# Block-sparse attention with a Fourier mixer: the mask's factors in one room, GpSimd adds the last units, and three smaller moves

## The chip, the cores and the metric

The kernel runs on one core of one Trainium2 chip. A core has TensorE (PE, with its weight loads shown as PEld), VectorE (DVE), ScalarE (ACT), GpSimd (POOL) and SyncE (SP), which issues most of the DMAs. The metric is the device time of one launch in microseconds (us), as the median of several executions; lower is better. One further execution was recorded by the hardware profiler. Its span is the time from its first to its last instruction, and all times inside the kernel are counted from the start of that span.

## What is computed

Attention over 4 batches of 8 heads, 768 positions and 64 elements a head, with a mask on blocks of 32 x 32 positions; then a Fourier mixer over the joined heads.

```python
scores = scale * np.matmul(q, k.transpose(0, 1, 3, 2))
mask = np.abs(blk_i - blk_j) <= window            # + first/last block rows and columns
for qb in range(n_blocks):
    for kb in sampled_blocks[qb]:                  # 3 random blocks for each block of queries
        mask[qb*block:(qb+1)*block, kb*block:(kb+1)*block] = True
attn = softmax(np.where(mask, scores, -1e9));  x = attn @ v      # (4, 8, 768, 64)
x = x.transpose(0, 2, 1, 3).reshape(4, 768, 512)
u = x + np.real(np.fft.fft(np.fft.fft(x, axis=1), axis=2))
un = (u - mean) / np.sqrt(var + 1e-6)
out = u + np.maximum(un @ w_ch1, 0) @ w_ch2        # w_ch1 512 x 2048, w_ch2 2048 x 512
```

The mask depends on the random blocks, so it is built on the chip from `sampled_blocks`.

## The kernel before

**Units, slots and batches.** Two heads make a pair; there are 16 pairs, four in each batch. A pair has 12 units: two halves of 384 queries by six chunks `c` of 128 keys. Two units make a slot, six slots a pair and 24 slots a batch. The function `slot(sl)` (96 attention slots and then the rest) issues a slot's work for all engines in program order. In each slot TensorE computes the scores of two units (`scores`, L570, 4 matmuls each), ACT takes the exponential to `e` (`weigh`), and a slot or two later TensorE multiplies `e` with the values (`values`, L633). The loop also puts in work of other kinds from queues: `short` (turning the next q and k with TensorE, L503; placing finished outputs, `xt` L657; totals), `apart` and `late` (the mixer of the batch before). Where these go is decided while the program is written out: the code keeps modelled times of each engine (`when`, `busy`) and of each PSUM bank (`free`, `give`), and takes the first item that is ready by this model. So a change of one cost, bank or queue can move other instructions too.

**The mask, in two ways.** In the first, TensorE adds a large negative number to forbidden scores: the mask as a product of two bf16 factors, `of_k` (24 rows that say which block a key is in, kept twice at rows 0 and 64) and `off_q`, accumulated into the scores' PSUM bank (L580, "factor products"); then one exponential (L590) gives `e`. In the second, ACT takes the exponential in place (L593) and DVE multiplies it by a uint8 mask (L595). The first is used for the whole first batch and on, until `go()` ends it (L1311 to 1313) when the first mixer's channels begin. The uint8 mask is computed in batch 0 by 12 `mask_step`s (L355 to 364): one matmul of the two factors over 24 rows into bank "m" (L361), and a cast by ACT (L363), one in each slot from 4 to 15.

**Where the factors are.** They are made in two tiles of the tag "acc", which later hold the sums of `e`. At the end of slot 19, `keep_factors` (L475 to 480) has POOL copy both into room 2 of a set of big rooms (`big0` to `big5`), for use from slot 20 on. Until then the six rooms are a ring for weight chunks: each of 32 chunks of 512 KB is loaded by SP (`w_load`, L441) into room `i % 6`, then split for rounding by two ACT instructions (L450, L453) and five DVE ones (L454 to L462), 1.42 chunks a slot. A load needs its room's former chunk to be rounded.

**Sums of the exponentials.** In batch 0 TensorE adds `e` over the keys (`add_up`, L701). From pair 4 on, `gather` adds each unit to a running sum `acc` for its half: POOL in two halves of 384 elements (L619), or DVE in one instruction of 768 (L614), chosen by the model's times; only units masked by TensorE may go to DVE. For those units `gather` is called in `values`, a slot after the exponential; for the others right after the DVE multiply. In the second slot of the next pair at the latest `total` (L715) sums both halves over the keys with TensorE, into bank "t", and DVE adds the result to the batch's sums.

**Turning.** `turn` (L486 to 519) turns q or k of a pair with TensorE (L503) into a PSUM bank, "t" or "m", which `turn_on` names, and ACT or DVE copies it out.

**The last outputs.** For the last batch, `outputs` (L1124 to 1190) forms each 128-row block `m` of the outputs by 256-column products (L1151), that DVE adds to `xA` and `xB` (L1158). `plus(b1, p5)` and `plus(b0, ...)` complete the two column halves of a block of the second sequence half, and `plus(a1, p3)` the first half's. `store` (L1096 to 1101) then writes whole rows of 512 columns from SP, as one or two DMAs by the order in which the rows lie.

Of the kernel before, what the change touches and what calls it, by code (L numbers as in the profile page):

```python
# [102 lines left out]
def kernel(  # L103
# [101 lines left out]

    HOP = 0.1

    pairs = [(b, j) for b in range(B) for j in range(NP)]
    loaded, v_of = {}, {}

# [113 lines left out]
                                pattern=pat)  # L324


    at_k = acc_p.tile([P, 2, 2 * HS], BF16, tag="acc", name="at_k")
    at_q = acc_p.tile([P, 2, 2 * HS], BF16, tag="acc", name="at_q")
    of_k, off_q, keep_q = at_k[:, 0, :], at_q[:, 0, :], at_q[:, 1, :]

    nc.vector.memset(of_k, 0.0)
    nc.vector.memset(off_q, 0.0)

    def twice(t):
        nc.vector.tensor_copy(out=t[D:D + NB, :], in_=t[0:NB, :])
# [20 lines left out]
    twice(off_q)  # L356
    def mask_step(i):

        half, c = divmod(i, C)
        m, at = ps_m.tile([P, 512], FP32, tag="m", name="m"), bank("m")  # L360
        nc.tensor.matmul(m[:, 0:HS], of_k[0:NB, c * P:(c + 1) * P],  # L361
                         keep_q[0:NB, half * HS:(half + 1) * HS], start=True, stop=True)
        nc.scalar.copy(out=mask[:, c, half * HS:(half + 1) * HS], in_=m[:, 0:HS])  # L363
        give(at, busy("ACT", 0.5, busy("PE", 0.2) + HOP))


    def table_s(src, dst, t):
# [64 lines left out]
                              ap=[[2 * cols, P], [1, 2 * WN]])  # L432
                wchunks.append((src, w_sb[:, row, col:col + WN]))
    wraw = {}
    ROOMS = 6
    def room(i, shape, name, dtype=FP32):
        return big.tile(shape, dtype, tag=f"big{i}", name=name)

    def w_load(i):
        t = room(i % ROOMS, [P, 3 * WN], "wraw", U32)  # L440
        nc.sync.dma_start(out=t[:, 0:2 * WN].bitcast(I32), in_=wchunks[i][0])  # L441
        wraw[i] = t

# [25 lines left out]

    by_pe = set()
    factors = {"at": (of_k, off_q)}

    def keep_factors():  # L475

        kept = room(2, [P, 2, S], "factors", BF16)
        for a, t in enumerate(factors["at"]):
            nc.gpsimd.tensor_copy(out=kept[:, a, :], in_=t)
        factors["at"] = kept[:, 0, :], kept[:, 1, :]  # L480

    turned, e_of, acc_of, o_of, sums_of, x_of, sp_of = {}, {}, {}, {}, {}, {}, {}
    s_at, e_at, e_free, oT_at, acc_at = {}, {}, {}, {}, {}

    def turn_on(n, a, half):
        return "m" if n > NP and (a, half) == (0, 1) else "t"  # L486

    def turn(n, a, half):

# [63 lines left out]
    def scores(us):  # L553

        n, w = divmod(us[0], UP)
        half = w // C
        qT, kT = turned[n, 0], turned[n, 1]
        queries = slice(half * HS, (half + 1) * HS)
        got = []
        for u in us:  # L560
            c = u % C
            s = ps_s.tile([P, 2, 512], FP32, tag="s", name="s")
            got.append((u, s))
            if n < NP or (factors["at"] and True):
                by_pe.add(u)
            busy("PE", 0.72, max(e_at.get(u - SLOT, 0.0), z_at[u % 2]))
            s_at[u] = when["PE"] + HOP
            for i in range(2):
                rows = slice(D * i, D * i + D)
                nc.tensor.matmul(s[:, i, 0:HS], kT[rows, c * P:(c + 1) * P], qT[rows, queries],  # L570
                                 start=True, stop=u not in by_pe)
        for u, s in got:
            if u not in by_pe:
                continue
            c, (at_k, at_q) = u % C, factors["at"]
            busy("PE", 0.25)
            s_at[u] = when["PE"] + HOP
            for i in range(2):
                rows = slice(D * i, D * i + D)
                nc.tensor.matmul(s[:, i, 0:HS], at_k[rows, c * P:(c + 1) * P], at_q[rows, queries],  # L580
                                 start=False, stop=True)
        return got

    def weigh(u, s):
        n, w = divmod(u, UP)
        half, c = divmod(w, C)
        e = ep.tile([P, 2, HS], FP32, tag="e", name="e")
        e_of[u] = e
        if u in by_pe:
            nc.scalar.activation(out=e, in_=s[:, :, 0:HS], func=ACT.Exp, scale=scale)  # L590
            e_at[u] = busy("ACT", 0.8, max(s_at[u], e_free.pop(u - 2 * SLOT, 0.0))) + HOP
        else:
            nc.scalar.activation(out=s[:, :, 0:HS], in_=s[:, :, 0:HS], func=ACT.Exp, scale=scale)  # L593
            m = mask[:, c, half * HS:(half + 1) * HS].rearrange("p (o s) -> p o s", o=1)
            nc.vector.tensor_tensor(out=e, in0=s[:, :, 0:HS], in1=m.broadcast_to([P, 2, HS]),  # L595
                                    op=ALU.mult)
            e_at[u] = busy("DVE", 0.97, busy("ACT", 0.8, s_at[u]) + HOP) + HOP
            if n >= NP:
                gather(u)

    def gather(u):


        n, w = divmod(u, UP)
        half, c = divmod(w, C)
        if c == 0:
            return
        if c == 1:
            acc_of[n, half] = acc_p.tile([P, 2, HS], FP32, tag="acc", name="acc")
        acc, e = acc_of[n, half], e_of[u]  # L610
        start = e_of[u - 1] if c == 1 else acc
        at = max(e_at[u], acc_at.get((n, half), 0.0))
        if u in by_pe and factors["at"] and max(when["DVE"], at) + 1.0 < max(when["POOL"], at) + 2.9:
            nc.vector.tensor_tensor(out=acc, in0=start, in1=e, op=ALU.add)  # L614
            acc_at[n, half] = busy("DVE", 1.0, at) + HOP
        else:

            for i in range(2):
                nc.gpsimd.tensor_add(out=acc[:, i, :], in0=start[:, i, :], in1=e[:, i, :])  # L619
            acc_at[n, half] = busy("POOL", 2.9, at) + HOP  # L620
        e_free[u] = acc_at[n, half]

    def values(u):
        n, w = divmod(u, UP)
        half, c = divmod(w, C)
        e = e_of[u]
        busy("PE", 0.75, e_at[u])
        vt = v_of[n]
        if c == 0:
            o_of[n, half] = ps_o.tile([P, HS], FP32, tag="o", name="o")  # L630
        o = o_of[n, half]
        for i in range(2):
            nc.tensor.matmul(o[D * i:D * i + D, :], vt[:, i, c, :], e[:, i, :],  # L633
                             start=(c == 0), stop=(c == C - 1))
        if u in by_pe and n >= NP:
            gather(u)
        if c == C - 1:
            if half == 1:
                v_of.pop(n)
            oT = sum_p.tile([P, HS], FP32, tag="oT", name="oT")  # L640
            if in_blocks(n):
                nc.vector.transpose(out=oT, in_=o_of.pop((n, half)))
                oT_at[n, half] = busy("DVE", 0.5, when["PE"] + HOP) + HOP
# [299 lines left out]
    def mixer(b, xA, xB):  # L943
# [149 lines left out]
            if r == NF // 4 - 1:  # L1093
                store(half, m)

        def store(half, m):  # L1096
            x = (xA, xB)[half]
            for p0, cnt, rows in _rows(out[b], T * half + m):
                nc.sync.dma_start(out=rows, in_=x[p0:p0 + cnt, m, :])
            if m == T - 1:  # L1100
                finished.add((b, half))

# [34 lines left out]
        def outputs(r, m, after):  # L1137
# [43 lines left out]
               in1=u.rearrange("p (o d) -> p o d", o=1).broadcast_to([P, 2, DH]), op=ALU.add)  # L1181
            busy("DVE", 0.7)
            plus(b1, p5)
            ahead(2)
            plus(b0, product(ps_s, "s", a22, rights[4]))
            if r == 1:
                store(1, m)
            ahead(3)
            p3 = product(ps_m, "m", o_s[m, 4], block(r, 1, 1))
            plus(a1, p3)  # L1190
            if r == 1:
                store(0, m)
            ahead(4)

        fl = [[("tm"[h == 1 and m != 1], lambda h=h, m=m: un_flip(h, m), 0.6, 0.55, 0.0)
               for m in range(T)]
# [105 lines left out]
    def begin(b):  # L1302
# [7 lines left out]

        def go():  # L1311
            late.extend(rest)
            factors["at"] = None
        apart.append(("-", go, 0.0, 0.0, 0.0, hold))

    def rest():
# [7 lines left out]
        return True  # L1324

    def w_loads():
        while state["got"] < min(len(wchunks), state["w"] + ROOMS):
            w_load(state["got"])
            state["got"] += 1

# [5 lines left out]
    def slot(sl):  # L1336
# [23 lines left out]
        got = scores(units) if sl < B * SB else ()  # L1360
        if paired and len(due) == 2:
            sum_up()
        for u, ps in got:
            weigh(u, ps)
        if BY_VECTOR <= n + 1 < len(pairs):
            for at, fn, args in ((0, squares, (n + 1, 0)), (1, flip_blocks, (n + 1, 0)),
                                 (2, in_order, (n + 1,)), (4, flip_blocks, (n + 1, 1)),
# [50 lines left out]
        if sl == 0:  # L1418
            short.append(("t", 0.0, lambda: turn(0, 1, 1)))
        if sl == 1:  # L1420
            short.append(("t", 0.0, lambda: turn(0, 0, 1)))
        if phase == 0 and 4 <= sl < 4 + 2 * C:
            short.append(("m", 0.0, lambda: mask_step(sl - 4)))
        if r > 0 and 0 < phase and not needed.intersection(map(id, short)) and once("mixing", phase):
            begin(phase - 1)
        left = SB * (phase + (0 if r == 0 else 1)) + 1 - sl
# [24 lines left out]
            item[2]()  # L1451
        w_loads()
        w_steps(sl)
        if sl == SB - 5:
            keep_factors()
        if sl >= 4 and sl % 2 == 0:
            table_step()

# [139 lines left out]
```

## Time and profile before

| | us |
|---|---|
| median of 3 executions | 1077.72 (1076.29 to 1078.42) |
| the profiled execution | 1078.02 |
| its span | 1075.9 |
| mean granted TensorE clock | 0.991 |
| factor products L580 on the kept factors, x108 | 14.0 busy, 6.1 idle before them |
| factor products L580 on the first tiles, x80 | 9.8 |
| mask matmuls L361, x12 | 4.0 |
| ACT mask casts L363, x12 | 5.9 |
| POOL adds L619, x150 and x44 | 152.1 and 48.2 |
| DVE adds L614, x21 | 20.8 |
| DVE mask multiplies L595, x98 | 89.1 |

The page gives the busy time of each engine, the span in 40 slices (26.9 us each, in tenths; the row PEclk is the granted clock of TensorE), the DMA queues, the chain of work that ended last, the groups of instructions by line, and the DMA issues. A group's line names the engine, the operation, output and inputs, how often it ran, its busy time and the mean of one, and then the idle time of the engine just before these instructions with what ended it. Queries of the trace give the waits, the timeline of a stretch, and the engines' busy time by stretch. The time of the profiled execution is about 2.1 us longer than its span.

### The profile page before, as it was taken

Reading aid. Unit: us, or ns where it says so; the run is one execution under the profiler, and the core shown is the slowest. Engines: PE = TensorE matmul, PEld = TensorE weight load, DVE = VectorE, ACT = ScalarE, POOL = GpSimd, SP = SyncE. Lnnn points to the kernel's source line nnn. Section 1 sums busy time; section 2 is a strip of 40 time slices with the busy share of each in tenths; the row PEclk is TensorE's granted clock in tenths of the full one; section 3 lists DMA queues with packets and bytes.
Section 4 is the critical chain, followed back from the end, with each engine's and each line's share of the span. In section 5 each row is a group of like instructions: output and inputs, shape, how many; then the busy total and the mean of one; then the engine's idle time right before and its main releaser. Section 6 shows DMA issues by size and latency. Waiting matters only on the chain.

```text
span 1075.9 us, 12388 instructions
## 1 busy us (share of the span) xinstructions
PE 1042.7 (97%) x4378; PEld 536.5 (50%) x4378; DVE 665.4 (62%) x1226; ACT 375.7 (35%) x742; POOL 231.1 (21%) x258
## 2 busy tenths in 40 slices
PE   8999898999999999999999999999999999999996
PEld 4433344444355555444444555443444555568575
DVE  5899694776771644664568446565556364675663
ACT  5998664563411202353352202243330302210210
POOL 1000080332700001256455001354630001000000
PEclk9999898999999999999999999999999999999998
DMA  7757230220100001222211000221000001000001
GB/s 225 222 176 240 58 71 15 45 45 16 29 1 1 0 1 30 59 38 42 54 27 33 0 1 10 69 40 31 15 8 8 0 1 30 30 1 1 1 18 44
DMA packets 120481, 46.65 MB, mean 43 GB/s; under 512 B 108110, under 2 KB 113244, under 8 KB 120412
## 3 DMA queue, kind: packets, MB, share of 16 engines
q1 hardware_dynamic: 118524, 44.99, 17.0%
q10 hardware_dynamic: 1856, 0.79, 0.3%
q8 instruction: 36, 0.59, 0.2%
q14 instruction: 33, 0.27, 0.1%
q0 software_dynamic: 32, 0.01, 0.0%
HBM read 37.11 MB, written 6.29 MB: 40 GB/s over the span
## 4 chain that ended last, share of the span: by engine, by line
PE 88%; DVE 7%; ACT 2%; issue 2%; POOL 1%; DMA 0%; ACTq 0%; DVEq 0%; POOLq 0%
PE y L1088 22%; PE z L1032 15%; PE s L570 12%; PE o L633 10%; PE yp L1032 7%; PE yy L1151 6%; PE xp L1032 4%; PE zp L842 2%; PE sp L701 1%; PE s L580 1%; PE zp L814 1%; PE utp L957 1%; DVE x L743 1%; PE sp L715 1%; PE tp L503 1%
## 5 line engine op out<-in xcount | busy, mean ns | idle before, releaser
L619 POOL TENSOR_TENSOR acc<-acc,e 128x384 f32<-128x384 f32 x150 | 152.1, 1050 | 85.3 <-DVE e L595 83.2
L570 PE MATMUL s<-qT,kT 64*128 64x384 f32 x768 | 154.4, 518 | 3.3 <-DVE e L595 1.9
L633 PE MATMUL o<-e,vr 128*64 128x384 f32 x768 | 142.8, 500 | 0.0
L1088 PE MATMUL y<-w_sb,hB 128*128 128x512 f32 x288 | 128.6, 596 | 1.4 <-DVE x L1091 1.4
L1088 PE MATMUL y<-w_sb,hA 128*128 128x512 f32 x288 | 129.2, 595 | 0.0
L1091 DVE TENSOR_TENSOR x<-y,x 128x512 f32<-128x512 f32 x72 | 49.7, 690 | 121.4 <-PE y L1088 121.2
L595 DVE TENSOR_TENSOR e<-s,mask 128x768 f32<-128x768 f32 x98 | 89.1, 950 | 56.8 <-ACT s L593 46.9
L593 ACT ACTIVATE s<-s 128x768 f32<-128x768 f32 x98 | 74.3, 792 | 93.3 <-PE s L570 93.0
L570 PEld LDWEIGHTS s<-qT,kT 64*128 64x128 f32 x768 | 64.3, 187 | 79.0 <-issue 24.1
L1032 PE MATMUL z<-unT,t 128*128 128x384 f32 x256 | 93.1, 486 | 0.7 <-DVE hA L1037 0.7
L590 ACT ACTIVATE e<-s 128x768 f32<-128x768 f32 x94 | 71.6, 814 | 47.7 <-PE s L580 33.9
L1088 PEld LDWEIGHTS y<-w_sb,hB 128*128 128x128 f32 x288 | 53.3, 190 | 67.3 <-issue 64.0
L905 POOL TENSOR_SCALAR st<-st 128x1 f32<-128x1 f32 x24 | 8.8, 365 | 355.2 <-DVE st L904 355.1
L1037 DVE TENSOR_TENSOR hA<-z,hA 128x384 f32<-128x384 f32 x64 | 35.7, 557 | 79.8 <-PE z L1032 79.8
L633 PEld LDWEIGHTS o<-e,vr 128*64 128x64 f32 x768 | 48.3, 137 | 71.6 <-issue 68.6
L1088 PEld LDWEIGHTS y<-w_sb,hA 128*128 128x128 f32 x288 | 53.1, 190 | 61.5 <-issue 58.4
L619 POOL TENSOR_TENSOR acc<-e 128x384 f32<-128x384 f32 x44 | 48.2, 1115 | 127.1 <-PE sp L715 93.6
L1041 ACT ACTIVATE hA<-hA 128x384 f32<-128x384 f32 x64 | 33.5, 523 | 119.0 <-DVE hA L1037 118.6
L1032 PEld LDWEIGHTS z<-unT,t 128*128 128x128 f32 x256 | 48.6, 190 | 35.0 <-DVE hA L1037 1.3
L1041 ACT ACTIVATE hB<-hB 128x384 f32<-128x384 f32 x64 | 33.5, 523 | 87.0 <-DVE hB L1037 87.0
L1052 ACT COPY hA<-xp 128x384 f32<-128x384 f32 x32 | 15.3, 478 | 107.0 <-PE xp L1032 107.0
L1032 PE MATMUL z<-t,w_sb 128*128 128x384 f32 x128 | 46.7, 488 | 0.9 <-DVE t L994 0.9
(206 smaller groups left out, 1439.2 us busy)
## 6 DMA issues: line engine op xcount, KB each, us to landing
wraw<-in_moe_w_ch_dram SPq DMA_DIRECT2D x32, 512.0 KB
vr<-in_v_dram SPq DMA_DIRECT2D x30, 192.0 KB
qb<-in_q_dram SPq DMA_DIRECT2D x44, 96.0 KB
kb<-in_k_dram SPq DMA_DIRECT2D x44, 96.0 KB
x<-oT SPq DMA_DIRECT2D x192, 12.0 KB
out_dram<-x SPq DMA_DIRECT2D x16, 128.0 KB
out_dram<-x SPq DMA_DIRECT2D x8, 256.0 KB
qr<-in_q_dram SPq DMA_DIRECT2D x24, 64.0 KB
```

Of the source, the lines that this page charges most:

```text
L570: nc.tensor.matmul(s[:, i, 0:HS], kT[rows, c * P:(c + 1) * P], qT[rows, queries], start=True, stop=u not in by_pe)
L590: nc.scalar.activation(out=e, in_=s[:, :, 0:HS], func=ACT.Exp, scale=scale)
L593: nc.scalar.activation(out=s[:, :, 0:HS], in_=s[:, :, 0:HS], func=ACT.Exp, scale=scale)
L595: nc.vector.tensor_tensor(out=e, in0=s[:, :, 0:HS], in1=m.broadcast_to([P, 2, HS]), op=ALU.mult)
L619: nc.gpsimd.tensor_add(out=acc[:, i, :], in0=start[:, i, :], in1=e[:, i, :])
L633: nc.tensor.matmul(o[D * i:D * i + D, :], vt[:, i, c, :], e[:, i, :], start=(c == 0), stop=(c == C - 1))
L1032: nc.tensor.matmul(to, a[:, k, :], c[:, k, :], start=(k == 0), stop=(k == ND // 2 - 1))
L1037: tt(out=to, in0=ps, in1=a, op=ALU.add)
L1041: nc.scalar.activation(out=h, in_=h, func=ACT.Relu)
L1088: nc.tensor.matmul(y, hs[0, half][:, l, m * P:(m + 1) * P], w2_sb[:, 4 * r + l, :], start=(l == 0), stop=(l == 3))
L1091: nc.vector.tensor_tensor(out=x[:, m, :], in0=y, in1=x[:, m, :], op=ALU.add)
L1151: nc.tensor.matmul(ps, a[:, k, :], c[k // 2][:, k % 2, :] if isinstance(c, list) else c[:, k, :], start=(k == 0), stop=(k == 3))
```

## The change

Five parts:

1. **Factors.** `of_k`, `off_q` and `keep_q` are made in one bf16 tile in room 2 from the start, and stay there. `keep_factors` with its two copies is gone. The weight ring has five rooms, 0, 1, 3, 4 and 5. Rows of `keep_q` that hold nothing are set to zero.
2. **Last units.** Of units masked by TensorE, the last two of a pair (chunks 4 and 5 of the second half) are always added by POOL, and as soon as their exponential is issued. A queue `to_gather` keeps the sums in order.
3. **Last outputs.** In `outputs` the product for `b0` comes behind the one for `a1`, and so does its store. In the very last outputs the columns 256 to 511 of the second half's block are stored as soon as `b1` is complete, and the columns 0 to 255 in two stores of 128 columns, one from SP and one from ACT's queue.
4. **Mask products.** The mask matmul runs over 64 rows rather than 24 and stands right behind a slot's factor products, in slots 3 to 20 without every third; ACT's cast comes behind that slot's exponentials.
5. **Turning.** The second half of q of pairs 0 and 1 is turned in bank "m", not "t". The old rule named pairs above 4, and those are not turned by `turn`.

```diff
-    at_k = acc_p.tile([P, 2, 2 * HS], BF16, tag="acc", name="at_k")
-    at_q = acc_p.tile([P, 2, 2 * HS], BF16, tag="acc", name="at_q")
-    of_k, off_q, keep_q = at_k[:, 0, :], at_q[:, 0, :], at_q[:, 1, :]
+    factors = room(2, [P, 3, S], "factors", BF16)
+    of_k, off_q, keep_q = (factors[:, i, :] for i in range(3))
...
+    nc.vector.memset(keep_q, 0.0)
...
     def mask_step(i):
...
-        nc.tensor.matmul(m[:, 0:HS], of_k[0:NB, c * P:(c + 1) * P],
-                         keep_q[0:NB, half * HS:(half + 1) * HS], start=True, stop=True)
-        nc.scalar.copy(out=mask[:, c, half * HS:(half + 1) * HS], in_=m[:, 0:HS])
-        give(at, busy("ACT", 0.5, busy("PE", 0.2) + HOP))
+        nc.tensor.matmul(m[:, 0:HS], of_k[0:D, c * P:(c + 1) * P],
+                         keep_q[0:D, half * HS:(half + 1) * HS], start=True, stop=True)
+        done = busy("PE", 0.17) + HOP
+
+        def keep_it():
+            nc.scalar.copy(out=mask[:, c, half * HS:(half + 1) * HS], in_=m[:, 0:HS])
+            give(at, busy("ACT", 0.5, done))
+        return keep_it
...
-    ROOMS = 6
+    W_ROOMS = (0, 1, 3, 4, 5)
     def w_load(i):
-        t = room(i % ROOMS, [P, 3 * WN], "wraw", U32)
+        t = room(W_ROOMS[i % len(W_ROOMS)], [P, 3 * WN], "wraw", U32)
...
-    def keep_factors():
-
-        kept = room(2, [P, 2, S], "factors", BF16)
-        for a, t in enumerate(factors["at"]):
-            nc.gpsimd.tensor_copy(out=kept[:, a, :], in_=t)
-        factors["at"] = kept[:, 0, :], kept[:, 1, :]
...
-        return "m" if n > NP and (a, half) == (0, 1) else "t"
+        return "m" if n < 2 and (a, half) == (0, 1) else "t"
...
         if u in by_pe:
             nc.scalar.activation(out=e, in_=s[:, :, 0:HS], func=ACT.Exp, scale=scale)
             e_at[u] = busy("ACT", 0.8, max(s_at[u], e_free.pop(u - 2 * SLOT, 0.0))) + HOP
+            if n >= NP:
+                to_gather.append(u)
+
+            if w >= UP - SLOT:
+                gather_to(u)
         else:
...
+            gather_to(u)
             if n >= NP:
                 gather(u)
+
+    def gather_to(u):
+        while to_gather and to_gather[0] <= u:
+            gather(to_gather.popleft())
...
-        if u in by_pe and factors["at"] and max(when["DVE"], at) + 1.0 < max(when["POOL"], at) + 2.9:
+        if u in by_pe and masks["by_pe"] and w < UP - SLOT and max(when["DVE"], at) + 1.0 < max(when["POOL"], at) + 2.9:
...
     def values(u):
...
-        if u in by_pe and n >= NP:
-            gather(u)
+        gather_to(u)
...
+            ends = r == 1 and after is None
+            if ends:
+                store(1, m, slice(DH, DM))
             ahead(2)
-            plus(b0, product(ps_s, "s", a22, rights[4]))
-            if r == 1:
-                store(1, m)
-            ahead(3)
             p3 = product(ps_m, "m", o_s[m, 4], block(r, 1, 1))
             plus(a1, p3)
             if r == 1:
                 store(0, m)
+            ahead(3)
             ahead(4)
+            plus(b0, product(ps_s, "s", a22, rights[4]))
+            if ends:
+                store(1, m, slice(0, P))
+                store(1, m, slice(P, DH), nc.scalar)
+            elif r == 1:
+                store(1, m)
...
+        keep_mask = None
+        if 3 <= sl < 3 + 3 * C and sl % 3 != 1:
+            keep_mask = mask_step(2 * (sl // 3 - 1) + sl % 3 // 2)
         for u, ps in got:
             weigh(u, ps)
+        if keep_mask:
+            keep_mask()
...
-        if phase == 0 and 4 <= sl < 4 + 2 * C:
-            short.append(("m", 0.0, lambda: mask_step(sl - 4)))
...
-        if sl == SB - 5:
-            keep_factors()
```

`store` takes the columns and the queue as arguments. The two kernels' orders of instructions, set side by side, show what follows from this: 200 factor products (L580) where there were 188, 94 exponentials to `e` become 100 and 98 DVE mask multiplies 92, POOL adds to `acc` go from 150 to 158 (and the first ones of a half from 44 to 42), the DVE adds that start from `acc` from 21 to 17. TensorE's order differs in the slots up to 55 and in the last outputs; the mixer's channels begin in slot 51 rather than 46. The sums of pair 4's second half go POOL, POOL, DVE, POOL, POOL (chunks 1 to 5; before: four by POOL and the last by DVE), and pair 5's total moves from slot 37 to 36.

More of the change, by code (lines that the diff above doesn't have):

```diff
@@ L206, with room @@
     HOP = 0.1
+    def room(i, shape, name, dtype=FP32):
+        return big.tile(shape, dtype, tag=f"big{i}", name=name)
     pairs = [(b, j) for b in range(B) for j in range(NP)]
@@ L434 @@
     wraw = {}
-    ROOMS = 6
-    def room(i, shape, name, dtype=FP32):
-        return big.tile(shape, dtype, tag=f"big{i}", name=name)
+    W_ROOMS = (0, 1, 3, 4, 5)
     def w_load(i):
-        t = room(i % ROOMS, [P, 3 * WN], "wraw", U32)
+        t = room(W_ROOMS[i % len(W_ROOMS)], [P, 3 * WN], "wraw", U32)
         nc.sync.dma_start(out=t[:, 0:2 * WN].bitcast(I32), in_=wchunks[i][0])
@@ L463, in w_round @@
         busy("DVE", 3.0, busy("ACT", 1.2))
-    by_pe = set()
-    factors = {"at": (of_k, off_q)}
-    def keep_factors():
-        kept = room(2, [P, 2, S], "factors", BF16)
-        for a, t in enumerate(factors["at"]):
-            nc.gpsimd.tensor_copy(out=kept[:, a, :], in_=t)
-        factors["at"] = kept[:, 0, :], kept[:, 1, :]
+    by_pe, to_gather = set(), deque()
+    masks = {"by_pe": True}
     turned, e_of, acc_of, o_of, sums_of, x_of, sp_of = {}, {}, {}, {}, {}, {}, {}
@@ L563, in scores @@
             got.append((u, s))
-            if n < NP or (factors["at"] and True):
+            if n < NP or masks["by_pe"]:
                 by_pe.add(u)
@@ L574, in scores @@
                 continue
-            c, (at_k, at_q) = u % C, factors["at"]
+            c = u % C
             busy("PE", 0.25)
@@ L579, in scores @@
                 rows = slice(D * i, D * i + D)
-                nc.tensor.matmul(s[:, i, 0:HS], at_k[rows, c * P:(c + 1) * P], at_q[rows, queries],
+                nc.tensor.matmul(s[:, i, 0:HS], of_k[rows, c * P:(c + 1) * P], off_q[rows, queries],
                                  start=False, stop=True)
@@ L1094, in channels, with store @@
                 store(half, m)
-        def store(half, m):
+        def store(half, m, cols=slice(0, DM), queue=nc.sync):
             x = (xA, xB)[half]
-            for p0, cnt, rows in _rows(out[b], T * half + m):
-                nc.sync.dma_start(out=rows, in_=x[p0:p0 + cnt, m, :])
+            for p0, cnt, rows in _rows(out[b][:, cols], T * half + m):
+                queue.dma_start(out=rows, in_=x[p0:p0 + cnt, m, cols])
             if m == T - 1:
@@ L1312, in go @@
             late.extend(rest)
-            factors["at"] = None
+            masks["by_pe"] = False
         apart.append(("-", go, 0.0, 0.0, 0.0, hold))
@@ L1326, in w_loads @@
     def w_loads():
-        while state["got"] < min(len(wchunks), state["w"] + ROOMS):
+        while state["got"] < min(len(wchunks), state["w"] + len(W_ROOMS)):
             w_load(state["got"])
@@ L1420, in slot @@
         if sl == 1:
-            short.append(("t", 0.0, lambda: turn(0, 0, 1)))
-        if phase == 0 and 4 <= sl < 4 + 2 * C:
-            short.append(("m", 0.0, lambda: mask_step(sl - 4)))
+            short.append((turn_on(0, 0, 1), 0.0, lambda: turn(0, 0, 1)))
         if r > 0 and 0 < phase and not needed.intersection(map(id, short)) and once("mixing", phase):
```

## The prediction

> **What bounds the kernel now.** I read the page's busy table first, then its clock row, then what TensorE waited for, then a table by stage, then the timeline around the two longest waits.
>
> ```profile
> PE 1042.7 (97%) x4378; PEld 536.5 (50%) x4378; DVE 665.4 (62%) x1226; ACT 375.7 (35%) x742; POOL 231.1 (21%) x258
> PEclk9999898999999999999999999999999999999998
> PE 88%; DVE 7%; ACT 2%; issue 2%; POOL 1%; DMA 0%; ACTq 0%; DVEq 0%; POOLq 0%
> ```
>
> TensorE is busy for 97% of the span and is 88% of the chain that ended last. So only three things are on offer: its idle time (1075.9 - 1042.7 = 33.2 us, about 9 of them after the last matmul), the time it spends at half clock (slices 4 and 6 show an 8), and its own work. Which idle is worth something:
>
> ```profile
> PE s L580 <- POOL factors L479: 6.1, 1, 6.1
> PE sp L715 <- DVE acc L614: 3.8, 1, 3.8
> PE warm L306 <- POOL ident masks.py:199: 2.6, 1, 2.6
> PE xt L657 <- ACT unT L958: 2.0, 1, 2.0
> ...
> PE tp L503 <- ACT qT L512: 1.1, 1, 1.1
> ```
>
> (waiting instruction, releaser: total us, times, longest). Two single waits lead. By stage (stretch, its length, then PE, PEld, DVE, ACT, POOL busy, clock, DMA share, GB/s):
>
> ```profile
> 20.00:106.00 86.00, 84.64 (x568) 33.67 (x566) 79.07 (x166) 76.57 (x157) 0.00 (x0) 1.00 0.70 215
> 106.00:118.00 12.00, 5.85 (x28) 1.77 (x28) 4.38 (x12) 2.77 (x8) 1.59 (x2) 0.72 0.36 117
> 118.00:161.00 43.00, 42.16 (x273) 17.30 (x269) 37.68 (x60) 30.75 (x58) 21.60 (x16) 1.00 0.29 56
> 161.00:175.00 14.00, 10.16 (x43) 4.26 (x39) 12.38 (x17) 5.27 (x14) 2.27 (x2) 0.76 0.01 1
> 175.00:330.00 155.00, 151.22 (x699) 73.70 (x698) 101.79 (x169) 66.51 (x129) 46.98 (x48) 1.00 0.14 26
> ```
>
> Both waits stand in short stages with a clock of 0.72 and 0.76; around them it is 1.00. Up to 106 DVE (79.07 of 86) and ACT (76.57) are nearly as full as TensorE; after 330 only TensorE is. The first wait, on the timeline:
>
> ```profile
> 109.86 0.69 DVE L462 TENSOR_TENSOR w_sb<-w_sb,wraw 128x512 f32<-128x512 f32 x1
> 110.68 0.82 POOL L479 COPY factors<-at_k 128x768 bf16<-128x768 bf16 x1 [105.58 <-DVE w_sb L462]
> 111.45 0.83 POOL L479 COPY factors<-at_q 128x768 bf16<-128x768 bf16 x1
> 112.33 0.82 PE L580 MATMUL s<-factors 64*128 64x384 bf16 x4 [6.15 <-POOL factors L479]
> ```
>
> The copies go to room 2, which a weight chunk holds until its rounding ends; the products wait for the copies. The second wait:
>
> ```profile
> 150.38 10.24 POOL L619 TENSOR_TENSOR acc<-acc,e 128x384 f32<-128x384 f32 x6 [0.16 <-ACT e L590]
> 161.33 0.84 PE L715 MATMUL sp<-acc,pick 128*32 128x384 f32 x4
> 165.01 0.95 DVE L614 TENSOR_TENSOR acc<-acc,e 128x768 f32<-128x768 f32 x1
> 166.01 1.50 PE L715 MATMUL sp<-acc,pick 128*32 128x384 f32 x4 [3.84 <-DVE acc L614]
> ```
>
> The total of pair 4 needs both halves' sums. DVE adds the last unit of the second half, and has put it behind its other work: 165.01.
>
> **What the skill says.** The Trainium skill, "TensorE: Matmul & The Clock Gate", section Part 1: The HAM clock gate (the "warmup" mystery), has a clock that falls to half after an idle window of about 3.4 us and returns after a busy one. The trace agrees: the waits of 6.1 and 3.8 us are each followed by 6.8 us at half clock, the wait of 2.0 us (at 231) by none. "SBUF — State Buffer", section Who interferes with whom, has DVE with two SBUF inputs and GpSimd share a read port, each blocking the other. Here a GpSimd add takes 1.05 us in the mean (L619) and 10.24/6 = 1.71 beside DVE's adds. "DMA: Bandwidth & Descriptors", section Why a DMA increments its semaphore by 16 and not by 1, has the largest divisor up to 16 of the slowest dimension choose the number of DMA engines. A store of two 64-row parts would run on two: the last of them moves at a DMA share of 0.13 (2/16) between 1072 and 1074.
>
> **The change, part by part,** against the profiled run's 1078.02 us (span 1075.9).
>
> *Factors in their own room.* The two POOL copies go and with them the wait. From scores to factor products takes 1.39 us elsewhere, so these were due at 106.01 and came at 112.33: 6.32 lost. From there to the next scores took 5.17 us at half clock against 3.01 in an undisturbed slot: 2.16. Together -8.5. Next late would be the exponentials behind weight rounding on ACT, whose waits here are under 1 us. The extra memset (0.38 us like its sisters) falls into 0.67 us of DVE idle at 1.9.
>
> *Five weight rooms for six.* Each 512 KB load is issued one DVE rounding (3.05 us of DVE work) later. I compared each chunk's first ACT step with the end of the following load's data, which is when it would itself land now: most have 1 to 4 us to spare, chunk 15 has -1.06 (68.23 against 69.29), chunks 17, 21 and 24 under 0.5. So ACT stops 1 to 2 us near 68, and about 1.3 reaches TensorE, since this stage has little slack.
>
> *Mask products behind factor products.* One alone adds 0.26 us to TensorE's order (31.29 to 31.55); behind factor products it costs between their own spacing, 0.42/4 = 0.105 (28.28 to 28.70), and 0.26. I take 0.16, an estimate: 12 x 0.10 = -1.2 of TensorE time. The ACT cast (489 ns) goes behind the two exponentials. DVE and ACT being full, I credit half: -0.6.
>
> *First pairs' q halves in bank "m".* The 1.1 us wait of tp on qT at 17.88 goes; slot 2's exponential then queues behind rounding, so I count -0.5. Nothing of this is hidden by other work, but it is only worth as much as ACT follows. Rooms, masks and start: +1.3 for chunk 15, +0.6 for 17, 21 and 24, -0.6, -0.5: +0.8 up to 106. Bounds -2 and +4.
>
> *GpSimd adds the last two units of the second half.* On the old time base: POOL ends c2 at 153.8, DVE does c3 behind an already finished fold (155.4), POOL does c4 (155.5 to 158.9, two contended adds of 1.71) and c5 to 162.3. The second half is ready at 162.3 instead of 165.96. Scores that began at 167.44 begin at 163.2: -4.2. TensorE then idles under 1 us, so the half-clock loss goes too: in the four steps after 166 it was 0.73 + 1.33 + 0.30 + 0.28 = 2.64, of which I count 1.9 as order there changes. Together -6.1, bounds 0 and -7.5. Queued behind these adds on POOL are only the next half's adds.
>
> *Moves that follow.* Masking by TensorE runs three slots longer (200 factor products for 188): 3 x 0.42 us = +1.3; six DVE multiplies go, 0.95 each, beside TensorE. xt stands behind o instead of right after utp: of the 2.0 us I take -1.5. The mixer's channels begin at slot 51 instead of 46. For this replanning I add +1.0, bounds 0 and +3. From slot 56 on (about 330 us) the order is the same.
>
> *The last outputs.* The last DVE add ends at 1067.4, the last semaphore comes after 1073. The store that decides is that of two 64-row parts issued at 1065.68 (8.2 us to completion; an earlier one took 7.8), on two DMA engines; the 64-row stores behind it spread over 16. A 2 KB packet took 84 ns, 1 KB about 46, 512 B about 28. Before: 64 x 84 = 5.4 us per engine. Now the same rows go as 1 KB and two times 512 B: 64 x (46 + 56) = 6.5, the first part issued 0.5 earlier. The b0 product now comes last, its parts go out on two queues. Net +0.5; bounds -3.4 (the ACT queue's part runs beside) and +1.
>
> Sum: +0.8 - 8.5 - 6.1 - 1.5 + 1.3 + 1.0 + 0.5 = -12.5, so 1065.5 for a run such as the profiled one. The median stands 0.3 below that run: 1065.2.
>
> **The rivals.**
> 1. *As above*, 0.58; its own range 1061 to 1069.
> 2. *Only the copies' wait goes.* POOL's chain is slower than 10.24/6 suggests and pair 4's total still stops TensorE over 3 us, with the clock. For: 1.71 us is a mean beside DVE, and DVE is 12.38 of 14 busy there. Against: by the working above POOL ends at 162.3, 3.7 us before the DVE add did. 1065.2 + 6.1 = 1071.3; 0.17.
> 3. *More is gained*: TensorE runs at its own pace before 106 too, and the stores run side by side: -2 for +0.8, -3 for +0.5: 1065.2 - 6.3 = 1058.9; 0.08. Against it: DVE is 79.07 of 86.
> 4. *Slower: GpSimd as last adder makes later totals late.* In pairs 5 to 7 DVE could step in before; now it may not. Each late total costs 3.84 + 2.64 = 6.5 us as measured at pair 4. With pair 4's gain lost too (-12.5 + 6.1 = -6.4) one further late total is break-even and two make +6.6: 1084.3; 0.12. For: pair 5's total (slot 36) has one slot's room, some 8.5 us of TensorE work for 8.8 of adding. Against: the others have two slots or more, and 1075.9 - 231.1 leaves POOL mostly idle.
> 5. *A wash*, that one late total: 1078; 0.05.
>
> **How the numbers follow.** 0.2% (about 2.2 us) is what a measurement can tell from no change. Cases 1 to 3 are faster: 0.83; case 5 no change: 0.05; case 4 slower: 0.12. The likeliest gives 1065.2. The bounds of rooms, adds, replanning and stores reach down to about 1057 and up to 1074; that leaves out case 4, case 5 and the best of case 3, some 2 in 10.
>
> **What would show it.** Right: no wait on factors, and no 8 in slices 4 and 6 of the clock row; sp's wait on acc under 2 us near 162; 200 factor-product matmuls; ACT waiting on weight loads for 1 to 2 us near 68; xt's 2.0 us gone; about 7 us from the last DVE add to the end. Wrong: a new TensorE wait over 3 us between 150 and 330, above all sp on a GpSimd acc, or ACT waiting on loads throughout the first 106 us.

## The result and the profile after

The changed kernel takes 1064.69 us (median of 4, 1063.79 to 1065.37), the kernel before 1077.95 (median of 4). The ratio is 0.9879, with a 95% interval of 0.9862 to 0.9896: 13.3 us less. The profiled execution took 1064.52 us with a span of 1062.8. Its page, with the busy times, the clock row and the chain:

```profile
PE 1036.0 (97%) x4390; PEld 536.1 (50%) x4390; DVE 654.4 (62%) x1218; ACT 374.0 (35%) x742; POOL 235.5 (22%) x262
PEclk9999999999999999999999999999999999999998
PE 87%; DVE 4%; DMA 3%; ACT 2%; issue 1%; SPq 1%; POOL 0%; ACTq 0%; DVEq 0%
```

Only the last slice shows a lowered clock (an 8), and it fell at 1055.18, behind the last matmul (1050.65). DMA now has 3% of the chain, where it had 0%: by line, weight loads and the last stores. What TensorE waited for (waiting instruction, releaser: total us, times, longest):

```profile
PE s L569 <- ACT e L589: 4.7, 8, 2.2
PE s L569 <- DVE e L599: 3.3, 4, 1.3
PE warm L309 <- POOL ident masks.py:199: 2.6, 1, 2.6
```

Both leading waits of before, and xt's, are gone; the longest new one is 2.2 us. By stage (columns as in the prediction's table):

```profile
20.00:104.00 84.00, 79.89 (x547) 31.80 (x545) 77.01 (x162) 73.44 (x149) 0.00 (x0) 1.00 0.70 209
104.00:118.00 14.00, 13.64 (x94) 5.40 (x94) 12.29 (x28) 11.81 (x28) 0.00 (x0) 1.00 0.68 179
...
161.00:175.00 14.00, 14.00 (x72) 7.68 (x71) 6.08 (x6) 7.69 (x19) 3.20 (x3) 1.00 0.17 28
```

The two stages with the long waits are full. The first, before 104, has become worse: TensorE is busy for 95% of it (before 98%).

Since the two kernels compute the same scores in the same slots, the start of each slot's first score matmul can be compared. That gives a ledger with an entry for each stage, in which the gains and the losses stand apart:

| stage | before | after | change | predicted |
|---|---|---|---|---|
| start to slot 0 | 8.98 | 8.70 | -0.28 | |
| slots 0 to 20 | 95.63 | 95.18 | -0.45 | with the start +0.8 |
| slots 20 to 31 (factors) | 53.24 | 45.50 | -7.74 | -8.5 |
| slots 31 to 59 (pair 4's total and the new plan) | 307.61 | 299.80 | -7.81 | -6.1 - 1.5 + 1.3 + 1.0 = -5.3 |
| slot 59 to the last matmul | 601.45 | 601.48 | +0.03 | 0 |
| last matmul to the end | 9.00 | 12.16 | +3.16 | +0.5 |
| sum | 1075.9 | 1062.8 | -13.1 | -12.5 |

That the sum agrees to 0.6 us is luck in good part. Against the forecast, slots 31 to 59 gained 2.5 us more and the start up to slot 20 1.5 more, while the factors' stage gained 0.8 less and the end lost 2.7 more, and these misses cancel. The experiments take the stages one by one.

### The profile page after: what moved, and what is told of

Same layout as the page of the kernel before. It is cut to its first block, busy times and chain, and to the rows that moved or that the text cites. A ratio compares the mean times of both kernels' runs of the same rounds, so it can differ in the third digit from the quotient of the medians.

```text
span 1062.8 us, 12409 instructions
## 1 busy us (share of the span) xinstructions
PE 1036.0 (97%) x4390; PEld 536.1 (50%) x4390; DVE 654.4 (62%) x1218; ACT 374.0 (35%) x742; POOL 235.5 (22%) x262
## 4 chain that ended last, share of the span: by engine, by line
PE 87%; DVE 4%; DMA 3%; ACT 2%; issue 1%; SPq 1%; POOL 0%; ACTq 0%; DVEq 0%
PE y L1096 23%; PE z L1040 15%; PE s L569 11%; PE o L642 10%; PE yp L1040 7%; PE yy L1159 7%; PE xp L1040 4%; PE zp L850 2%; DMA wraw<-in_moe_w_ch_dram 1%; DMA out_dram<-x 1%; PE s L579 1%; PE zp L822 1%; PE sp L723 1%; PE utp L965 1%; PE sp L709 1%
## 5 line engine op out<-in xcount | busy, mean ns | idle before, releaser
L628 POOL TENSOR_TENSOR acc<-acc,e 128x384 f32<-128x384 f32 x158 | 159.3, 1043 | 94.1 <-DVE e L599 75.1
L599 DVE TENSOR_TENSOR e<-s,mask 128x768 f32<-128x768 f32 x92 | 83.9, 952 | 57.8 <-ACT s L597 48.0
L597 ACT ACTIVATE s<-s 128x768 f32<-128x768 f32 x92 | 69.9, 792 | 87.6 <-PE s L569 87.0
L589 ACT ACTIVATE e<-s 128x768 f32<-128x768 f32 x100 | 75.9, 812 | 35.1 <-PE s L579 30.0
L1040 PE MATMUL xp<-unT,w_sb 128*128 128x384 f32 x128 | 47.2, 492 | 0.0
```

Source lines behind the costliest of these rows:

```text
L1040: nc.tensor.matmul(to, a[:, k, :], c[:, k, :], start=(k == 0), stop=(k == ND // 2 - 1))
```

## The experiments

The kernel before took 1076.9 to 1077.7 us (medians) beside these runs. Below, "slots 0 to 20" and the like are the stages of the ledger in a run's profile. The stage of slots 0 to 20 varies from run to run of the same order: 95.2 to 97.0 us in eight profiles with five rooms and the changed masks and turns. The last section shows what this goes with. A stage is read from one profile of each run.

**Last outputs as before.**

```diff
-            ends = r == 1 and after is None
-            if ends:
-                store(1, m, slice(DH, DM))
             ahead(2)
+            plus(b0, product(ps_s, "s", a22, rights[4]))
+            if r == 1:
+                store(1, m)
+            ahead(3)
             p3 = product(ps_m, "m", o_s[m, 4], block(r, 1, 1))
...
-            ahead(3)
             ahead(4)
-            plus(b0, product(ps_s, "s", a22, rights[4]))
-            if ends:
-                store(1, m, slice(0, P))
-                store(1, m, slice(P, DH), nc.scalar)
-            elif r == 1:
-                store(1, m)
```

> The changed kernel with the last outputs of before (part 3 undone). Comparing the two traces slot by slot, the changed kernel reaches its last matmul 16.3 us earlier and ends only 13.1 us earlier, so theory A is that part 3 costs the 3.2 us in between: from the last matmul's end to the span's end 8.9 us instead of 12.1, all before it as in the changed kernel, time 1064.7 - 3.2 = 1061.5. Rival B, that the end just varies with how the DMA engines happen to be busy: 11 to 12 us again and a time within 1 us of 1064.7.

Measured: 1062.90 us, and 8.99 us from the last matmul to the end (9.00 in the kernel before). Theory A holds for the stage. The median gained 1.8 rather than 3.2; in the profiled run slots 0 to 20 took 96.54 us, 1.36 more than in the changed kernel's profile, since a stall of 2.7 us near 70 brought half clock with it, of which more below.

**One store for b0.**

```diff
-                store(1, m, slice(0, P))
-                store(1, m, slice(P, DH), nc.scalar)
+                store(1, m, slice(0, DH))
```

> The changed kernel, but the last 256 columns go out in one store from SP instead of two stores of 128 columns from SP and ACT. Theory A1: what costs is that a store of two 64-row parts, which moves on two DMA engines, is issued behind the last add; then 64 packets of 1 KB at 46 ns (2.9 us) stand for 128 of 512 B at 27 ns (3.5 us) and the end is 11 to 12 us behind the last matmul, time 1063.8 to 1064.8. Theory A2: what costs is the cut into columns and ACT's first DMA issue (1.38 us); then 9 to 9.5 us and about 1062.

Measured: 1063.93 us, end after 9.94 us: by the stage between the two theories, nearer A2, though the median lies in A1's range. Against the order of before, b0 last and its block stored in two column halves cost 9.94 - 8.99 = 0.95 us. The rest is in how b0 is stored.

**Both last stores from SP.**

```diff
-                store(1, m, slice(P, DH), nc.scalar)
+                store(1, m, slice(P, DH))
```

> The changed kernel with both last stores of 128 columns from SP, none from ACT. Known: with one store of 256 columns from SP the end is 9.9 us behind the last matmul, with the two stores 11.2 to 12.2. Theory A, the cut is what costs (twice as many packets, each 27 ns for 512 B against 46 for 1 KB): 10.5 to 11 us, 0.5 to 1.2 less than with ACT's queue. Theory B, ACT's queue costs (its issue takes 1.38 us against 0.55): 9.9 to 10.3 us.

Measured: 1064.21 us, end after 10.03 us, so B: the cut alone costs 0.1. With ACT's queue the end came after 11.2 to 12.2 us in seven profiles: 1.2 to 2.1 for that queue. Why it takes longer stays open: its issue takes 1.38 us, but SP's second issue in this run took 1.32. The medians of these two and of the changed kernel lie within 0.8 us; it is the stage that tells them apart. The timeline of the changed kernel's end, and its DMA share by stretch:

```profile
1050.69 0.42 DVE L1166 TENSOR_TENSOR x<-yy,x 128x256 f32<-128x256 f32 x1 [1.30 <-PE yy L1159]
1051.15 1.38 ACTq L1107 DMA_DIRECT2D out_dram<-x  x1
```

```profile
1054.00:1056.00 2.00, 0.00 (x0) 0.00 (x0) 0.00 (x0) 0.00 (x0) 0.00 (x0) 0.79 0.11 22
1056.00:1058.00 2.00, 0.00 (x0) 0.00 (x0) 0.00 (x0) 0.00 (x0) 0.00 (x0) 0.50 0.14 36
1058.00:1060.00 2.00, 0.00 (x0) 0.00 (x0) 0.00 (x0) 0.00 (x0) 0.00 (x0) 0.50 0.10 29
```

Six microseconds run at a share of 0.10 to 0.14, about two engines of 16 (0.125). The trace's packets: the last stores, issued at 1051.1, have their first packet of 512 B at 1054.9; SP's last one ends at 1059.2, ACT's at 1060.4. The store of `b1` was issued at 1048.9 and had its first packet at 1050.1, after 1.2 us rather than 3.8. What holds the later ones back is not shown.

**The second half's rows first.** On top of the last outputs as before:

```diff
-            plus(a0, product(ps_m, "m", a12, block(r, 1, 0)))
+            ends = r == 1 and after is None
+            if not ends:
+                plus(a0, product(ps_m, "m", a12, block(r, 1, 0)))
...
             if r == 1:
                 store(1, m)
             ahead(3)
+            if ends:
+                plus(a0, product(ps_m, "m", a12, block(r, 1, 0)))
             p3 = product(ps_m, "m", o_s[m, 4], block(r, 1, 1))
```

> The last outputs of before (part 3 undone), and in the very last block the second product of a0 moves behind b0's, so that the store of the second half's rows on two DMA engines starts one product (1.7 us) earlier and the stores on 16 engines come last. Theory A: the two-engine store sets the end: 8.9 - 1.7 = 7.2 us from the last matmul to the end, time about 1061.2. Rival B: the last stores set the end: 8.5 to 9 us, 1062.9.

Measured: 1060.19 us, end after 7.16 us: theory A. The store on two engines is issued at 1048.71, three microseconds ahead of the last matmul's end, and a share near two of 16 engines (0.08 here) is left in the last line only:

```profile
1052.00:1054.00 2.00, 0.00 (x0) 0.00 (x0) 0.14 (x1) 0.00 (x0) 0.00 (x0) 1.00 0.26 55
1054.00:1056.00 2.00, 0.00 (x0) 0.00 (x0) 0.00 (x0) 0.00 (x0) 0.00 (x0) 0.66 0.54 163
1056.00:1058.00 2.00, 0.00 (x0) 0.00 (x0) 0.00 (x0) 0.00 (x0) 0.00 (x0) 0.50 0.08 28
```

**Five rooms in the kernel before.**

```diff
-    ROOMS = 6
+    W_ROOMS = (0, 1, 3, 4, 5)
```

> The kernel before with five rooms for the weights (0, 1, 3, 4, 5), and nothing else: the factors are still copied by POOL at slot 19. Theory A: the stall was the wait for room 2, so the copies run at once and slot 20 takes about 5 us instead of 12.9, with no half clock behind it (-7.7 us); and ACT waits about 3 us for a weight chunk near 69, of which 2 to 2.5 reach TensorE: 1077.9 - 7.7 + 2.2 = 1072.4. Rival B: the copies themselves are late, the room doesn't matter: 1078 to 1080. Rival C: five rooms cost nothing, and what the changed kernel lost near slot 13 comes from the moved mask products: 1070.2.

Measured: 1070.39 us. Slots 20 to 31 take 44.79 us, 8.45 less than before, though the copies are still there: they waited for the room. Slots 0 to 20 take 97.28, 1.65 more, and the waits of ACT show why:

```profile
ACT wraw L450 <- DMA wraw<-in_moe_w_ch_dram: 2.1, 1, 2.1
```

TensorE stands still for 1.24 us there (at 70.6), where it had no such gap before. So A holds, and C, whose total is met, falls by the stages. The total is lower than A's for another reason: pair 4's total waited 3.84 us as before, but the half clock behind it lasted 3.41 us, not 6.83, and slots 31 to 59 took 306.38 us, not 307.61.

**Six rooms in the changed kernel.**

```diff
-    W_ROOMS = (0, 1, 3, 4, 5)
+    W_ROOMS = (0, 1, None, 3, 4, 5)
...
+        at = W_ROOMS[i % len(W_ROOMS)]
+        t = spare_w if at is None else room(at, [P, 3 * WN], "wraw", U32)
...
+    spare_w = xp.tile([P, 3 * WN], U32, tag="xB", name="wraw")
```

> The changed kernel with six rooms for the weights: the sixth is the second xB tile, which is free until the second batch. Theory A: ACT's wait of about 3 us for a chunk near 69 goes, slot 13 begins 2 us earlier and half of it or more stays: 1062.7 to 1063.7. Rival B: DVE is full there and takes it back by slot 20: 1064.7 within 0.5.

Measured: 1060.67 us, 4.0 less, more than theory A gave. Slots 0 to 20 take 92.11 us. The changed kernel's timeline at chunk 15, and then what TensorE waited for in the first 110 us with six rooms:

```profile
68.55 0.66 ACT L456 ACTIVATE wraw<-wraw 128x512 f32<-128x512 uint32 x1 [3.09 <-DMA wraw<-in_moe_w_ch_dram]
...
70.50 1.61 PE L569 MATMUL s<-qT,kT 64*128 64x384 f32 x8 [2.19 <-ACT e L589]
```

```profile
PE s L570 <- ACT e L590: 1.5, 5, 0.7
```

The chunk is late, its ACT step holds up the exponentials behind it in the queue, and these the next scores. With the sixth room no such wait exceeds 0.7 us.

**Masks and turns as before, with five rooms and with six.**

```diff
-        if 3 <= sl < 3 + 3 * C and sl % 3 != 1:
-            keep_mask = mask_step(2 * (sl // 3 - 1) + sl % 3 // 2)
...
+        if phase == 0 and 4 <= sl < 4 + 2 * C:
+            short.append(("m", 0.0, lambda: mask_step(sl - 4)))
...
-        return "m" if n < 2 and (a, half) == (0, 1) else "t"
+        return "m" if n > NP and (a, half) == (0, 1) else "t"
```

> The changed kernel with the mask products and turns of before (parts 4 and 5 undone: mask matmul over 24 rows from the queue, q halves in bank t). Theory A: before 104 us ACT and DVE set the pace, so the 0.1 us that each of 12 mask matmuls costs more and the 1.1 us wait of the turn are made up again within a few slots: slot 20 begins at 104 to 105.5 (changed: 103.9, with 104.7 to 105.4 in other runs of the same order) and the time is within 1 us of 1064.7. Rival B: TensorE's order counts in full, 1.2 + 1.1 us: slot 20 at 106 or later, time 1067.

> Six rooms for the weights, and masks and turns as before (parts 4 and 5 undone). With five rooms these parts were worth nothing that shows. Theory A: the weights' wait hid their gain; with six rooms slots 0 to 20 take 92.1 us with parts 4 and 5 and about 95.3 without (95.6 in the kernel before): time 1060.7 + 3.2 = 1063.9. Rival B: six rooms alone bring the 3 to 4 us, parts 4 and 5 are worth nothing here either: 1060.7 within 0.7.

Measured: 1064.65 us with five rooms, the changed kernel's own time; 1063.41 with six, against 1060.67. Slots 0 to 20 take 97.30 and 95.62 us.

With six rooms theory A holds. Parts 4 and 5 are worth 95.62 - 92.11 = 3.5 us in these slots, of which 0.76 comes back in slots 20 to 31 (44.77 without, 45.53 with): the last mask matmul stands there now, and four matmuls of a turn have moved from slot 19 to slot 20. From slot 0 to slot 31 the trace takes 140.38 us without these parts and 137.65 with them; TensorE is busy for 1.6 us less and idle for 1.1 less, the turn's wait of 1.12.

With five rooms theory A has the total, but not its reason, ACT and DVE at their limit, since that would hold with six rooms too; and slot 20 begins at 105.80, behind its 104 to 105.5. With parts 4 and 5 TensorE reaches slot 13 earlier and waits there longer for chunk 15: 2.2 to 3.2 us in the eight profiles, 1.09 without. So the weights' wait hides the gain. The two parts were not undone one at a time.

**The sums as before.**

```diff
-            if w >= UP - SLOT:
-                gather_to(u)
...
-        if u in by_pe and masks["by_pe"] and w < UP - SLOT and max(when["DVE"], at) + 1.0 < max(when["POOL"], at) + 2.9:
+        if u in by_pe and masks["by_pe"] and max(when["DVE"], at) + 1.0 < max(when["POOL"], at) + 2.9:
...
-        gather_to(u)
+        if u in by_pe and n >= NP:
+            gather(u)
```

> The changed kernel with the sums of before (part 2 undone: DVE may add the last units, and each is added a slot after its exponential). Theory A: pair 4's total is late again by 3 to 4 us, half clock follows, and slots 31 to 59 take 7.8 us longer: 1072.5. Rival B: with the factors in time the total comes in time by itself, and the gain behind slot 31 is from the new plan of the other parts: 1064 to 1066.

Measured: 1072.19 us, slots 31 to 59 in 306.63, theory A. The waits are those of before:

```profile
PE sp L714 <- DVE acc L613: 3.8, 1, 3.8
...
PE xt L656 <- ACT unT L957: 2.0, 1, 2.0
```

This run has 188 factor products again. So xt's wait and the three more masked slots also belong to part 2: its modelled times make the new plan.

**The last units by DVE, in POOL's place.** The modelled time stays POOL's, so that the plan is kept:

```diff
+        elif u in by_pe and masks["by_pe"] and w >= UP - SLOT:
+            nc.vector.tensor_tensor(out=acc, in0=start, in1=e, op=ALU.add)
+            acc_at[n, half] = busy("POOL", 2.9, at) + HOP
```

> The changed kernel with its plan unchanged, but the last two units of pairs 4 to 7 are added by DVE at the same place in the program as POOL adds them now. Theory A, it is the engine that matters: on DVE the adds queue behind the mixer's folds and pair 4's total is late by over 2.5 us again, with half clock: 1068 to 1072. Rival B, it is the earlier place and the new plan that matter: DVE's add takes 0.95 us where POOL's two take 2.1 to 3.4, the total is ready as early or earlier: 1064 to 1065.5.

Measured: 1064.30 us, slots 31 to 59 in 299.18 (changed: 299.80). Rival B: at this place the engine does not matter. DVE's timeline before the change, and in this run:

```profile
161.95 0.55 DVE L787 TENSOR_TENSOR sa<-sa 128x384 f32<-128x384 f32 x1
162.53 1.23 DVE L788 TENSOR_TENSOR sa<-sa 128x384 f32<-128x384 f32 x1
163.69 1.08 DVE L787 TENSOR_TENSOR e<-e 128x128 f32<-128x128 f32 x1
164.80 0.29 DVE L788 TENSOR_TENSOR e<-e 128x128 f32<-128x128 f32 x1
```

```profile
147.48 0.94 DVE L623 TENSOR_TENSOR acc<-acc,e 128x768 f32<-128x768 f32 x1
148.53 2.02 DVE L626 TENSOR_TENSOR acc<-acc,e 128x768 f32<-128x768 f32 x2
150.47 1.75 DVE L777 TENSOR_TENSOR sd<-x 128x1536 f32<-128x1536 f32 x1
```

Before, the add (165.01) stood behind the mixer's folds in DVE's queue. Issued right behind its exponential it stands ahead of them, and DVE has both last units by 150.5.

**POOL, but a slot later.**

```diff
-            if w >= UP - SLOT:
-                gather_to(u)
```

> The changed kernel with POOL as the adder of the last units, but each is added a slot after its exponential, as the kernel before did. With DVE in POOL's place at the early place the gain stayed, so theory A is that the place in the queue decides, not the engine: POOL's queue holds nothing but adds, so a slot later costs what the two contended adds take beyond the time to the total, 0.5 to 2.5 us of waiting at pair 4's total: 1065 to 1068. Rival B, the engine alone is enough: no wait over 0.5 us at the totals, slots 31 to 59 within 0.5 us of 299.8. Rival C, the early place is all: the wait is over 3 us with half clock, 1070 to 1072.

Measured: 1067.85 us (1065.68 to 1068.76), slots 31 to 59 in 302.89, with 3.41 us at half clock behind the wait: theory A. The timeline of POOL and TensorE:

```profile
143.28 12.33 POOL L626 TENSOR_TENSOR acc<-acc,e 128x384 f32<-128x384 f32 x8 [0.15 <-ACT e L589]
...
156.97 0.85 PE L721 MATMUL sp<-acc,pick 128*32 128x384 f32 x8 [2.19 <-ACT x L664]
```

POOL's last add ends at 155.61. The total then waits for ACT's copy of x: ACT stood at an exponential until POOL had read the `e` buffer that it needed, and the copy was queued behind. So a late add can stop TensorE in two ways, by its sum and by the buffer it keeps; here the buffer came last.

**Six rooms and the second half first.** The edits of those two runs together, on the changed kernel.

> The changed kernel with six rooms for the weights and the last outputs as in the run with the second half first. If the two gains (six rooms: 1064.7 to 1060.7; last outputs: 1064.7 to 1060.2) come from separate stages they add: 1056.2, within 0.7. If both profit from the same thing, for one the DMA engines, 1058 or more.

Measured: 1056.45 us (1055.80 to 1056.90), a ratio to the kernel before of 0.9799 (0.9785 to 0.9812). The two gains add, as they come from separate stages. This version beats both kernels; its page:

```profile
PE 1035.9 (98%) x4390; PEld 536.2 (51%) x4390; DVE 654.6 (62%) x1218; ACT 374.2 (35%) x742; POOL 235.9 (22%) x262
```

## Why the prediction was right, point by point

*Factors in their own room, -8.5.* Shown: 8.45 us in the run that only gives the room free. The changed kernel has -7.74 in this stage because parts 4 and 5 put 0.7 us more work into it, most of it the turn that moved out of slot 19.

*Rooms, masks and start, +0.8.* The profile has -0.73, a gain where I forecast a loss, and both terms were too small. The place was right to the chunk: number 15, ACT's wait at 68.55, which lasted 3.09 us and not 1 to 2. Of the near misses chunk 21 came late too: ACT waited 1.58 us for it. I priced the late chunk at 1.3 us on TensorE and three near misses at 0.6, 1.9 in all. Five rooms cost 1.65 in slots 0 to 20 of the kernel before and 4.0 of the median in the changed one, which gets to chunk 15 earlier and waits for it longer. And I credited masks and turns with half of their TensorE time, 1.1 together, since ACT and DVE are full. That halving was the wrong step: without the weights' wait they bring 2.7, somewhat more than the 1.2 and 1.1 that I had counted in full.

*Last units, -6.1.* The reason given, the add's place behind other work in DVE's queue, is what the runs show; that POOL should be the adder is not. DVE in the same place does as well. At the later place the adder made a difference: 302.89 with POOL, 306.63 with the sums as before, whose plan is another one too. The wait of 3.84 went, with its half clock, as forecast. I took 1.9 of the clock's loss; TensorE was busy 5.55 us within the 6.83 at half clock, so by my estimate half of that, 2.8, was lost. Two experiments with the same wait had 3.41 us at half clock, so how much there was to gain depended on where in the clock's steps the wait fell (last section).

*Moves that follow, -1.5 + 1.3 + 1.0.* Xt's wait of 1.99 went, and for the friction of the new plan nothing shows: -3.84 - 1.99 - 2.8 + 1.26 for 12 factor products is -7.4 of the -7.81 measured. The +1.0 was the mis-sized term.

*Last outputs, +0.5.* This step failed: +3.2. I had named the two DMA engines, but added packet times as one stream from the first store's issue. With b0 last, its stores can't be issued before the last add, and their packets begin 3.8 us after the issue. By the experiments 0.95 goes to b0 last and its two halves, 0.1 to the cut, 1.2 to 2.1 to ACT's queue. The bound I set above, +1, left out the largest of these: I had put the part on ACT's queue at nothing or at a gain, as running beside the rest.

*The rivals.* Late totals in pairs 5 to 7 did not occur: no wait of TensorE on acc is left in the changed kernel. That only the first wait would go is excluded by slots 31 to 59. That more is gained fell short at both of its places: the profile gained 0.7 us before slot 20, not 2, and the stores got slower. The run with six rooms and the second half first gets below its 1058.9 by other edits.

## What to carry to other kernels

Lay two traces side by side at matching instructions before you trust a total: here a gain of 2.5 us and a loss of 2.7 against the forecast cancelled. Put an add that a consumer waits for right behind its producer in its engine's queue: there it made no difference which of two engines did it (slots 31 to 59 in 299.80 and 299.18 us), and a slot later the stage took 302.89 and 306.63. At the end of this kernel it paid to issue the store that uses few DMA engines first (7.16 us against 8.99). And in a ring of loads look for a late chunk before you shorten the work that uses it: with five rooms the shorter work only waited longer.

## What was not expected of the hardware

The granted clock also fell at gaps shorter than the two of before, and not at all of them. Gaps of 1.99, 2.19, 2.31 and 2.39 us left it alone; gaps of 2.19, 2.53, 2.55, 2.58, 2.69 and 3.20 were each followed by 3.41 us at half clock; and the same gap of 3.84 at pair 4's total had 6.83 us of it in the kernel before and 3.41 in two experiments (3.83 and 3.84).

The clock record in the traces settles which. In each of the 14 profiles all changes of the clock lie on one grid of 3.41 us. In the kernel before they come at 7.71, 110.11, 116.94, 164.73 and 171.55, which is 0, 30, 32, 46 and 48 steps of 3.4133 us. The grid begins elsewhere in each run. TensorE's idle time, counted within the steps of this grid, tells the cases apart:

| run, place | gap | border of a step within it | most idle in one step | half clock |
|---|---|---|---|---|
| second half first, slot 13 | 68.17 to 70.70 | 68.18 | 2.53 | 3.41 |
| POOL a slot later, slot 13 | 68.49 to 71.07 | 69.07 | 2.00 | 3.41 |
| POOL a slot later, pair 4's total | 154.79 to 156.97 | none | 2.19 | 3.41 |
| both last stores from SP, slot 13 | 68.60 to 70.99 | 69.11 | 1.89 | none |
| changed kernel, slot 13 | 68.30 to 70.50 | 68.73 | 1.77 | none |
| five rooms before, pair 4's total | 154.74 to 158.58 | 156.42 | 2.16 | 3.41 |
| kernel before, pair 4's total | 162.17 to 166.01 | 164.73 | 2.55, then 1.29 | 6.83 |

All ten falls of the clock before the last matmul stand at the end of a step with 2.00 us or more of idle time; no step with 1.89 or less ended in one. Two steps already at half clock, with 1.29 and 2.21 us idle, were followed by another; every full one was followed by the full clock. So the same gap can cost a step, two or none, by where it falls. This rule is read from these 14 profiles; between 1.89 and 2.00 us they have no case.

The Trainium skill, "TensorE: Matmul & The Clock Gate", section Part 1: The HAM clock gate (the "warmup" mystery), has a window of 3.4 us that runs free of the kernel. The steps agree with that window; that a gap below 3.4 us drops the clock differs from it, and there the measurement decides.

Five rooms' stall at slot 13, 2.2 to 3.2 us, lies on this edge. The three profiles that kept the clock there have 95.18 to 95.54 us in slots 0 to 20, the five that lost it 96.41 to 97.04. The changed kernel's own profile is one of the three, so its ledger shows the better case.
